# Two-branch attention kernel: when single score tiles may run, when unit queries are loaded, when GpSimd's branch A work pauses

## The chip, the cores and the metric

The kernel runs on one core of one Trainium2 chip. The metric is device time in microseconds of one execution. TensorE multiplies matrices, VectorE (DVE) reduces and combines, ScalarE (ACT) evaluates exponents and copies, GpSimd (POOL) does elementwise work in SBUF, and SyncE (SP) issues most DMAs. Each engine works through its own instructions in the order in which the program lists them.

## What is computed

The reference mixes two attention branches over the same input x (2048 positions, width 512, 32 heads of 16) with a gate per position:

```python
x = A_x
g = _sigmoid((x * gate_w).sum(-1, keepdims=True))
a = _A_ref(x, A_wqkv, A_wo)   # 8 keys per position, at distances 0, 2, ..., 14
b = _B_ref(x, B_wq, B_wk, B_wv, B_wo)
return g * a + (1 - g) * b

# in _B_ref: 32 query heads share one key head and one value head
scores = jnp.einsum("bhqd,bkd->bhqk", q, k) * (Dh ** -0.5)
p = _softmax(scores, axis=-1)
o = jnp.einsum("bhqk,bkd->bhqd", p, v)
```

Branch B is full softmax attention, 32 heads of 2048 x 2048 scores; branch A looks at 8 earlier positions and is done mostly on GpSimd.

## The kernel before

**Units.** Branch B's queries are cut into 32 units, each of 512 queries and 4 heads. A unit is worked off in 16 steps, one for each tile of 128 keys, so that the second phase has 512 steps, `s` from 0 to 511, with `u, kt = divmod(s, 16)`. In a step, `exp_pair` (L568, L570) makes the scores of two heads in each of two PSUM banks `pe` and ScalarE exponentiates them into `pexp`; `weighted(s - 1)` (L578) multiplies the exponents of the step before with the values into the bank `po`.

**Fills.** The exponent is taken of a score less the maximum of its row, and the maxima are needed before the unit's first step. They come from a second pass of score matmuls, which run as fills between the other work. Each unit has 64 of them (2048 in all), each a matmul of 512 columns of keys with half of the array's rows, and a maximum by VectorE; one of these 64 is called a score below. They come in three forms:

- a **pair** (`fill_pair`, L384 and L413): two matmuls on the two halves of the array's rows, into the two-bank tile `pm` (`m2`), reduced in one VectorE instruction;
- a **single** (`fill_one`, L384 and L424): one of two scores of a slot, into the one-bank tile `ps` (`m1`); the other one stands in `half` until the next single. A single can also go through `pm`;
- in the first phase and in the row blocks below, **half forms** (L480, L506, L523), one matmul beside one of the projections.

`slots` lists what is left in order of units, `to_go()` counts it. When a unit's maxima are complete, `maxima_turn`, `shift_a`, `shift_c` and `shift_d` bring them, by way of VectorE and GpSimd (L530 to L541) and eight small DMAs (L556), into rows of the unit's queries.

**Loads of units.** `stack(u)` issues four DMAs on SP (L353, L354) that put a unit's queries from DRAM scratch into a buffer `qst`. There are eight buffers, later six; `home(v)` gives a unit's buffer and the unit whose steps must be over before. `stacked` holds for each unit loaded so far when the planner takes it to have landed (issue plus 5 us); `fillable()` asks that.

**Order.** All of it is one program that is written out in Python with a rough clock for each engine (`clk`, `pool`): the order of instructions on each engine is set by that planner, not by the chip. In each step of the second phase the loop issues: a load, if `s` is past the bound; the first exponent pair; a pair if `m2` is free (`fill_ready("m2", ...)`); a single if `singles(s)` allows it, except in the first step of most units; the second exponent pair; the weighted sum of the step before; then tasks that are due and GpSimd's work. `singles(s)` asks whether pairs in the remaining steps, and PER_ROW scores for each output row still to come, would be too few for what is left.

**Row blocks.** Output rows are made in blocks (`out_phase`, L862): eight rows at step 273, four at step 401 in this kernel. A block starts at the first step of a unit, when the queries' outputs are there and the `lead`, the units' worth of fills done less the units stepped through, is under LEAD = 3.0. The last four rows are spread over the last steps (L933).

**First phase.** `stream` runs the query projections and then branch A's projections: three column groups `gg` of 16 lumps `j`, each lump 12 products `i` on either half of the array's rows (L1185). The weights of the next group are split into two parts (`split_wa`: ScalarE writes `wah`, L111, GpSimd writes `wal`, L112). Two of the four splits are made in the last lump of a group, after its products 4 and 7. `done_mm` calls `run_pool()` after every third product; that issues GpSimd's branch A work (L642 to L702) until its clock is 2.5 us ahead, and with it the exponents and reductions of branch A on ScalarE and VectorE. GpSimd also adds up the projections' stages (L311).

Of the kernel before, what the change touches and what calls it, by code (L numbers as in the profile page):

```python
# [18 lines left out]
NJ = S // P  # L19
# [5 lines left out]
NU = NQB * NHG  # L25
# [8 lines left out]
GG = 3  # L34
GN = NAG * AN // GG
NB = 8
# [2 lines left out]
FMAX = 3.4028234e38  # L39
NH = NJ // 2  # L40
TO_END = 10
LEAD, M2S, M1S, E1S, PER_ROW = 3.0, 0.5, 0.3, 0.2, 20
M2H = 0.15
WB = 6

# [32 lines left out]
def gated_mix_kernel(ctx, tc, xt, wa, wk, wq, wo_a, wo_b, out):  # L78
# [21 lines left out]
    def home(v):  # L100

        return (v % NB, v - NB) if v < 2 * NB - 2 else ((v - NB) % (NB - 2), v - NB + 2)
# [11 lines left out]
    clk = {"pe": 0.0, "act": 0.0, "dve": 0.0}  # L114
# [229 lines left out]
    stacked, asked = [], set()  # L344
# [14 lines left out]
    slots = [(v, pr, t, kc) for kc in range(2) for v in range(2) for pr in range(2) for t in range(4)]  # L359
    slots += [(v, pr, t, kc) for v in range(2) for pr in range(2) for t in range(4) for kc in range(2, 4)]  # L360
    slots += [(v, pr, t, kc) for v in range(2, NU) for pr in range(2) for t in range(4) for kc in range(4)]
    half = []
# [4 lines left out]
    def fillable():  # L367
        return bool(half) or bool(slots) and slots[0][0] < len(stacked) and stacked[slots[0][0]] <= clk["pe"]
# [17 lines left out]
    def to_go():  # L386
        return 2 * len(slots) + len(half)
# [29 lines left out]
    def fill_one(dst=m1, key="m1"):  # L417
        if not half:
            v, pr, t, kc = slots.pop(0)
            half.extend([(v, pr, t, kc, 0), (v, pr, t, kc, 1)])  # L420
        v, pr, t, kc, odd = half.pop(0)
        m = unit_tile(v)
        max_mm(dst, v, pr, t, kc, odd)
        nc.vector.tensor_reduce(m[:, odd, pr, t, kc:kc + 1], dst, AX.X, ALU.max)  # L424
        free[key] = after("dve", after("pe", 0, T_R) + T_LAT, T_RED1) + 0.08
        filled(v, 1)
# [43 lines left out]
    def half_back():  # L470

        nc.sync.dma_start(q67.rearrange("p g x n -> p (g x n)").bitcast(F32), kd.rearrange("p g x n -> p (g x n)"))
        kcd[0] = q67
# [87 lines left out]
    pe, pexp, exped = [], {}, {}  # L561
# [63 lines left out]
    oa, p2, woh, wol = [], [], [], []  # L625
# [345 lines left out]

    def singles(s):

        return 2 * max(0, 16 * (NU - 1) - 16 - s) + PER_ROW * max(0, NJ - 4 - outs) < to_go()

    def fill_ready(key, slack):
        if fillable() and free[key] <= clk["pe"] + slack:
            clk["pe"] = max(clk["pe"], free[key])
            if key == "m1":
                fill_one()  # L980
            elif half and (not slots or half[0][0] < slots[0][0] or slots[0][0] >= len(stacked)):
                fill_one(m2[:, 0, :], "m2")
            elif slots:
                fill_pair(m2, "m2")
# [41 lines left out]
    def run_tasks():  # L1026
        for task in [t for t in tasks if t[0] <= clk["pe"]]:
            tasks.remove(task)
            task[1](*task[2])
# [158 lines left out]
    def done_mm(at):  # L1188
        nonlocal pool
        x, i = at  # L1190
        lump = lumps[x]
        if i % 3 == 2:
            run_tasks()
            if p2:
                run_pool()
        if x == last - 1 and i == 3 * C - 6:
            ended.add(1)
        if lump[0] == "a" and lump[2] == NJ - 1 and lump[1] + 1 < GG and i in (4, 7) and WB - C < 4:
            c = WB - C + (i == 7)
            if c < C:  # L1200
                split_wa(lump[1] + 1, c)
        if x == last and i in (2, 7):
            exp_pair(0, int(i == 7))
        if i < 3 * C - 1:
            return
        if lump[0] == "q":
            m = lump[1]
            if m == 12:
                gates()
            queries_post(m, eb[1 - x % 2])  # L1210
            free[f"e{1 - x % 2}"] = clk["act"]
            ahead_wa(0, m - 4)
        else:
            gg, j = lump[1:]
            a_post(gg, j, 2 if x == last else x % 2)
            if gg + 1 < GG:
                ahead_wa(gg + 1, j - 2)
# [20 lines left out]
    for s in range(NS + 1):  # L1238
        u, kt = divmod(s, NJ)
        if s == 16 * NB + 4:  # L1240
            half_back()
        if len(stacked) < NU and s > 16 * (home(len(stacked))[1] + 1):
            stack(len(stacked))
        if s < NS and kt == 0 and u not in shifted:
            while u not in shifted:
                clk["pe"] += 0.5
                run_tasks()
                if u not in shifted and left.get(u, 1):
                    assert pause(4)
        v = min(x[0][0] for x in (half, slots, [(NU,)]) if x)  # L1250
        need = left.get(v, NF // NU)
        steps = 16 * v - 6 - s
        short = need - 2.8 * max(0, steps) if v < NU else 0
        lead = (NF - to_go()) / 64 - s / 16
        order = (0, "m2", "later") if s else ()
        rows = 4 if outs else 8
        k, n = (outs + rows) // 4 - 1, C - (outs >= NJ - 4)
        if outs == NJ - 4:
            if s in (16 * NU - 40, 16 * NU - 32):
                blocks_out(outs + (s - 16 * NU + 40) // 8)  # L1260
            if to_go() <= 9 and not later_rows and "last" not in done:
                later_rows.append(spread(list(range(outs, NJ)), n))
            if short > 0 and steps < 2:
                pause(short)
        elif due or outs < NJ and s and kt == 0 and outs // NH in done and NHG * (k + 1) - 1 in shaped and (lead < LEAD or s >= 16 * (NHG * (k + 2) + 1)):
            if not due:
                prepare(outs, n)
                due.append(n)
            else:
                out_phase(list(range(outs, outs + rows)), due.pop(), kt == 1)  # L1270
                outs += rows
                order = (0, "m1", 2)
        elif short > 0 and steps < 2:
            pause(short)

        first = 0
        some = min(4, -(-(row_prods[0] - TO_END) // (NS + 1 - s)))
        order = list(order)
        while order:
            which = order.pop(0)  # L1280
            if which == "later":
                order = ["m1", 1] if free["e1"] > clk["pe"] - E1S else [1, "m1"]
                first = 0
            elif which == "m2":
                fill_ready("m2", M2S)
            elif which == "m1":
                if not later_rows and (kt or not s or u >= NU - 8) and singles(s):
                    first = half[0][4] if half else 0
                    fill_ready("m1", M1S)
            elif s < NS:  # L1290
                if which == 1:
                    spread_some(some)
                exp_pair(s, which % 2 or which // 2, which == 2, first)
        if s == NS:
            spread_some(some)
        if s:
            weighted(s - 1)
            if kt == 0 and s < NS:
                finish_a(u - 1, nc.gpsimd)
        run_tasks()  # L1300
        run_pool()
# [65 lines left out]
```

## Time and profile before

| | |
|---|---|
| median of 3 runs | 1475.75 us (1475.53 to 1475.97) |
| the profiled execution, own time | 1475.89 us |
| its span, first to last instruction | 1474.1 us |
| first phase, to the end of the first weighted sum | 273.5 us |
| busy VectorE, ScalarE, GpSimd | 81%, 87%, 68% |

A row of a group names line, engine, operation, what is written and read, shapes and count, then busy time and mean length, then the engine's idle time before it with what ended it. A row of a stretch has its ends, its length, the busy time and count of instructions of each engine (TensorE, its weight loads, and then those of the other engines that take part), the granted TensorE clock as a share of full speed, the share of the DMA engines that is busy, and GB/s. A row of the timeline has start, length, engine, line and operation. `SPq` and the like are an engine's queue, which waits or issues.

### The profile page before, as it was taken

What the parts mean: (1) busy time and instruction counts of PE and PEld (TensorE: products, weight loads), DVE (VectorE), ACT (ScalarE), POOL (GpSimd) and SP (SyncE); (2) the same over time, 40 slices, a digit from 0 to 9 for tenths busy, and PEclk for the clock granted to TensorE, in tenths of its full rate; (3) what the DMA queues carried; (4) which work ended last, traced back from release to release, by engine and by line L of the source; (5) the groups of instructions that cost most, each with busy time, mean ns of one, the idle gap of its engine ahead of it and who ended that gap; (6) DMA issues with size and microseconds to landing.
All of it is one profiled execution on the core that took longest, in us unless ns stands there. A gap on an engine that the chain in (4) does not pass through costs nothing.

```text
span 1474.1 us, 29007 instructions
## 1 busy us (share of the span) xinstructions
PE 1461.2 (99%) x10612; PEld 670.5 (45%) x10612; DVE 1191.0 (81%) x1880; ACT 1289.0 (87%) x1629; POOL 1001.4 (68%) x1753
## 2 busy tenths in 40 slices
PE   9999999999999999999999999999999999999998
PEld 5877777533333333333333377333333354333343
DVE  6978889858888888889898888888888888866612
ACT  5658888999999999999999988999999988999986
POOL 7853888778898988988878898788888231101121
PEclk9999999999999999999999999999999999999999
DMA  6752433211121111211211202021120000000110
GB/s 224 211 161 75 145 100 91 74 56 54 43 96 41 46 58 43 71 42 42 71 42 42 77 28 83 26 71 42 42 71 12 12 19 23 12 1 2 28 32 29
DMA packets 75263, 89.80 MB, mean 61 GB/s; under 512 B 56368, under 2 KB 56416, under 8 KB 70896
## 3 DMA queue, kind: packets, MB, share of 16 engines
q1 hardware_dynamic: 68176, 49.00, 11.7%
q0 software_dynamic: 6368, 37.90, 7.7%
q8 instruction: 83, 1.36, 0.4%
q10 hardware_dynamic: 576, 1.05, 0.2%
q14 instruction: 60, 0.49, 0.1%
HBM read 60.03 MB, written 27.35 MB: 59 GB/s over the span
## 4 chain that ended last, share of the span: by engine, by line
PE 97%; DVE 1%; ACT 1%; issue 1%; POOL 0%; DMA 0%; DVEq 0%; SPq 0%; ACTq 0%; POOLq 0%
PE po L578 34%; PE pe L568 23%; PE pe L1185 11%; PE pm L384 8%; PE ps L384 7%; PE pe L862 5%; PE pm L480 3%; PE po L480 2%; PE ps L480 2%; PE pm L933 1%; PE pe L208 1%; ACT pexp L570 1%; DVE qst L186 0%; POOL wal L112 0%; PE pe L753 0%
## 5 line engine op out<-in xcount | busy, mean ns | idle before, releaser
L570 ACT ACTIVATE pexp<-pe 128x1024 f32<-128x1024 f32 x1022 | 989.4, 1022 | 87.5 <-PE pe L568 84.3
L413 DVE TENSOR_REDUCE mx<-pm 128x2 f32<-128x1024 f32 x491 | 600.9, 1224 | 147.2 <-PE pm L384 136.4
L578 PE MATMUL po<-pexp,vst 128*32 128x512 f32 x4096 | 545.5, 605 | 0.0
L568 PE MATMUL pe<-qst,kst 64*128 64x512 f32 x1916 | 438.7, 451 | 0.8 <-ACT pexp L570 0.7
L568 PEld LDWEIGHTS pe<-qst,kst 64*128 64x128 f32 x1916 | 179.8, 183 | 480.4 <-ACT pexp L570 474.2
L424 DVE TENSOR_REDUCE mx<-ps 128x1 f32<-128x512 f32 x420 | 285.7, 680 | 0.0
L384 PE MATMUL pm<-kst,qst 62*128 62x512 f32 x967 | 196.7, 395 | 1.5 <-DMA qst<-qd 0.8
L642 POOL TENSOR_TENSOR pr<-aext 128x256 f32<-128x256 f32 x256 | 182.2, 739 | 4.5 <-DMA aext<-ad 4.2
L702 POOL TENSOR_TENSOR oa<-oa,av 128x256 f32<-128x256 f32 x224 | 164.0, 732 | 15.2
L384 PE MATMUL ps<-kst,qst 62*128 62x512 f32 x408 | 161.4, 396 | 0.3 <-DVE mx L424 0.2
L578 PEld LDWEIGHTS po<-pexp,vst 128*32 128x32 f32 x4096 | 80.5, 108 | 171.3 <-issue 162.6
L699 POOL TENSOR_TENSOR av<-aext,lg 128x256 f32<-128x256 f32 x224 | 139.3, 622 | 12.6
L506 ACT ACTIVATE dd<-pm 128x512 f32<-128x512 f32 x186 | 104.9, 604 | 23.4 <-PE pm L480 13.1
L1185 PE MATMUL pe<-wal,xh 64*128 64x512 f32 x376 | 118.8, 395 | 1.9 <-POOL wal L112 1.9
L1185 PE MATMUL pe<-wah,xh 64*128 64x512 f32 x376 | 119.8, 397 | 0.0
L1185 PE MATMUL pe<-wah,xl 64*128 64x512 f32 x376 | 118.9, 395 | 0.0
L605 POOL TENSOR_TENSOR rl<-rl,gate_t 128x16 f32<-128x16 f32 x31 | 6.9, 222 | 152.4 <-DVE rl L599 147.6
L384 PEld LDWEIGHTS pm<-kst,qst 62*128 62x128 f32 x967 | 94.0, 187 | 4.4 <-DMA qst<-qd 1.1
L648 POOL TENSOR_TENSOR tr<-pr 128x512 f32<-128x512 f32 x64 | 81.8, 1278 | 4.3
L506 ACT ACTIVATE pexp<-pm 128x512 f32<-128x512 f32 x120 | 68.2, 603 | 13.7 <-PE pm L480 9.5
L384 PEld LDWEIGHTS ps<-kst,qst 62*128 62x128 f32 x408 | 76.1, 187 | 6.4 <-DVE mx L424 3.4
L648 POOL TENSOR_TENSOR tr<-tr 128x256 f32<-128x256 f32 (+1 forms) x128 | 72.4, 565 | 8.8
(215 smaller groups left out, 1975.5 us busy)
## 6 DMA issues: line engine op xcount, KB each, us to landing
aext<-ad POOLq DMA_DIRECT2D x32, 1056.0 KB, 5.5
qst<-qd SPq DMA_DIRECT2D x60, 128.0 KB
ad<-stage SPq DMA_DIRECT2D x32, 240.0 KB
xraw<-xt SPq DMA_DIRECT2D x16, 256.0 KB
qd<-qhi SPq DMA_DIRECT2D x16, 256.0 KB
qd<-qlo SPq DMA_DIRECT2D x16, 256.0 KB
qst<-qd SPq DMA_DIRECT2D x60, 64.0 KB
qst<-ml SPq DMA_DIRECT2D x216, 2.0 KB
```

Of the source, the lines that this page charges most:

```text
L384: nc.tensor.matmul(dst, qst[home(v)[0]][b:b + 62, pr, t * P:(t + 1) * P], kst[b:b + 62, kc * 512:(kc + 1) * 512], start=True, stop=True)
L413: nc.vector.tensor_reduce(m[:, :, pr, t, kc], dst, AX.X, ALU.max)
L424: nc.vector.tensor_reduce(m[:, odd, pr, t, kc:kc + 1], dst, AX.X, ALU.max)
L506: nc.scalar.activation(d[:, odd], m2[:, odd, :], AF.Abs)
L568: nc.tensor.matmul(bank[:, odd, :], kst[b:b + 64, kt * P:(kt + 1) * P], qst[home(u)[0]][b:b + 64, pr, :], start=True, stop=True)
L570: nc.scalar.activation(e, bank, AF.Exp, scale=SCALE)
L578: nc.tensor.matmul(po[32 * i:32 * i + 32, :], vst[:, kt, :], pexp[s, i // 2][:, i % 2, :], start=(kt == 0), stop=(kt == NJ - 1))
L642: nc.gpsimd.tensor_mul(pr[:, k], q, e[:, o:o + NH, AC:2 * AC])
L648: nc.gpsimd.tensor_add(nx, cur[:, :, 0:n], cur[:, :, n:2 * n])
L699: nc.gpsimd.tensor_mul(av, e[:, o:o + NH, 2 * AC:].rearrange("p j (h d) -> p j h d", d=DH), lg[:, w].unsqueeze(3).to_broadcast([P, NH, AG, ...
L702: nc.gpsimd.tensor_add(ao, ao, av)
L1185: nc.tensor.matmul(front[2 if x == last else x % 2][0][:, b, :], l[h], r[h], start=(i == 0), stop=(i == 3 * C - 1))
```

## The change

Four edits, all in the planner:

- `singles(s)` says no while not all units are loaded and the scores ready for fills (of loaded units) are fewer than two for each step until the next unit's load is due and three steps more (`LAND`).
- In `fill_ready`, an odd score in `half` goes through `m2` by itself only if there is nothing left in `slots`, or the next slot's unit isn't loaded or hasn't landed by the planner's clock. Before, it also went so whenever it was of an older unit than the next slot.
- `done_mm` leaves `run_pool()` out from product 8 of lump 14 to product 8 of lump 15, in the first two of the three column groups.
- The loop issues a unit's load from `s >= 16 * (...)` on rather than `s > 16 * (...)`. PER_ROW goes from 20 to 21.

```diff
-LEAD, M2S, M1S, E1S, PER_ROW = 3.0, 0.5, 0.3, 0.2, 20
+LAND = 3
+LEAD, M2S, M1S, E1S, PER_ROW = 3.0, 0.5, 0.3, 0.2, 21
...
     def singles(s):
 
+        if len(stacked) < NU:
+            ready = len(half) + 2 * sum(x[0] < len(stacked) for x in slots[:16 * NB])
+            if ready < 2 * (16 * (home(len(stacked))[1] + 1) + LAND - s) + 1:
+                return False
         return 2 * max(0, 16 * (NU - 1) - 16 - s) + PER_ROW * max(0, NJ - 4 - outs) < to_go()
...
-            elif half and (not slots or half[0][0] < slots[0][0] or slots[0][0] >= len(stacked)):
+            elif half and (not slots or slots[0][0] >= len(stacked) or stacked[slots[0][0]] > clk["pe"]):
                 fill_one(m2[:, 0, :], "m2")
             elif slots:
                 fill_pair(m2, "m2")
...
         if i % 3 == 2:
             run_tasks()
-            if p2:
+            if p2 and not (lump[0] == "a" and lump[1] + 1 < GG and (lump[2] == NJ - 2 and i > 6 or lump[2] == NJ - 1 and i < 9)):
                 run_pool()
...
-        if len(stacked) < NU and s > 16 * (home(len(stacked))[1] + 1):
+        if len(stacked) < NU and s >= 16 * (home(len(stacked))[1] + 1):
             stack(len(stacked))
```

The matmuls, reductions and exponents themselves stay the same; which of them share a slot, and their order, changes.

## The prediction

> **What bounds the kernel now.** I read the page first (busy times, chain of waits), then a timeline of two ordinary steps of the second phase, then stretches of steps, then the few real stalls of TensorE.
>
> ```profile
> span 1474.1 us, 29007 instructions
> PE 1461.2 (99%) x10612; PEld 670.5 (45%) x10612; DVE 1191.0 (81%) x1880; ACT 1289.0 (87%) x1629; POOL 1001.4 (68%) x1753
> PE 97%; DVE 1%; ACT 1%; issue 1%; POOL 0%; DMA 0%; DVEq 0%; SPq 0%; ACTq 0%; POOLq 0%
> ```
>
> TensorE is busy for 99% and carries 97% of the chain. So a change must take matmuls' time, or TensorE's stalls, away. Next, one step of the second phase (start, length, instruction), and ScalarE in a later stretch:
>
> ```profile
> 420.13 0.50 PE L568 MATMUL pe<-qst,kst 64*128 64x512 f32 x2
> 420.47 0.40 PE L384 MATMUL pm<-kst,qst 62*128 62x512 f32 x2
> 420.70 0.41 PE L568 MATMUL pe<-qst,kst 64*128 64x512 f32 x2
> 420.95 0.39 PE L384 MATMUL ps<-kst,qst 62*128 62x512 f32 x1
> 421.27 1.06 PE L578 MATMUL po<-pexp,vst 128*32 128x512 f32 x8
> 422.27 0.50 PE L568 MATMUL pe<-qst,kst 64*128 64x512 f32 x2
> ...
> 1299.83 10.20 ACT L570 ACTIVATE pexp<-pe 128x1024 f32<-128x1024 f32 x10
> ```
>
> A step is two exponent pairs (pe), one fill pair (pm: two matmuls side by side in the array), one single (ps, alone), and the weighted sums (po). It took 2.14 us (420.13 to 422.27). The single occupies TensorE by itself for about a quarter of a microsecond, where a pair takes two scores in the same slot. In steps without a single ScalarE runs without a gap, ten exponents in 10.20 us. Stretches (length, TensorE, weight loads, VectorE, ScalarE, GpSimd, granted clock, DMA):
>
> ```profile
> 273.60:297.20 23.60, 23.60 (x167) 8.52 (x169) 20.34 (x25) 21.84 (x24) 17.78 (x30) 1.00 0.22 70
> 297.20:299.10 1.90, 1.90 (x16) 0.64 (x16) 1.56 (x3) 1.72 (x3) 1.66 (x4) 1.00 0.00 0
> 299.10:311.10 12.00, 11.43 (x74) 3.11 (x74) 1.46 (x4) 11.50 (x13) 9.04 (x16) 1.00 0.39 121
> 311.10:314.30 3.20, 2.40 (x17) 0.84 (x17) 1.24 (x2) 2.50 (x3) 3.12 (x7) 1.00 0.60 188
> 314.30:337.80 23.50, 23.50 (x167) 8.49 (x169) 20.76 (x25) 21.34 (x24) 17.03 (x43) 1.00 0.00 1
> 1276.40:1393.10 116.70, 116.60 (x814) 38.11 (x814) 76.20 (x74) 111.58 (x117) 7.65 (x17) 1.00 0.03 8
> ```
>
> The same stretches for the weighted sums alone (eight records a step) and for the fills alone:
>
> ```profile
> 273.60:297.20 23.60, 11.72 (x88) 1.73 (x88) 1.00 0.22 70
> 299.10:311.10 12.00, 6.39 (x48) 0.94 (x48) 1.00 0.39 121
> 1276.40:1393.10 116.70, 61.79 (x464) 9.12 (x464) 1.00 0.03 8
> ...
> 273.60:297.20 23.60, 8.38 (x33) 4.14 (x35) 1.00 0.22 70
> 299.10:311.10 12.00, 0.00 (x0) 0.00 (x0) 1.00 0.39 121
> 1276.40:1393.10 116.70, 23.13 (x116) 10.95 (x116) 1.00 0.03 8
> ```
>
> Numbered by the loop (the fills of step s run beside the weighted sum of s-1), 273.60 begins step 2. So 11 steps with pair and single, 2 to 12, take 23.60 (2.145 each; the 11 from 314.30 take 2.136); step 13, with a pair alone, takes 1.90; then **six steps, 14 to 19, have no fill at all** and still take 2.00 each, ScalarE's pace; and 58 steps in a row with a pair alone take 116.70/58 = 2.01. A pair is free in a run of such steps; a single costs 2.136 - 2.01 = 0.124 us there, 0.236 beside a lone 1.90. At 299.10 the eight loaded units were used up, since singles ran through steps 1 to 12; step 20, at 311.10, is the first with unit 8.
>
> **Part 1: held singles, the sooner load, and the half that waits.** Fills of the second phase:
>
> ```profile
> L413 DVE TENSOR_REDUCE mx<-pm 128x2 f32<-128x1024 f32 x464 | 568.1, 1224 | 142.4 <-PE pm L384 131.9 <-PE ps L384 6.8
> L424 DVE TENSOR_REDUCE mx<-ps 128x1 f32<-128x512 f32 x395 | 268.8, 680 | 0.0
> ...
> L424 DVE TENSOR_REDUCE mx<-pm x9: 691/692/693, 404.1 to 1149.5; 128x1 f32<-128x512 f32 x9
> ```
>
> From step 2 to step 480 there are 479 places for a pair. 464 are taken; 6 were empty, and 9 held a single only (pm, 128x1: an odd half of an old unit went first, which the edit of the fill rule stops). 464 + 6 + 9 = 479.
>
> At step 1 eight units are loaded and, counting back from 299.10, where they are used up (two scores in step 13, 33 in steps 2 to 12, three in step 1), 38 scores are ready. The new test asks at step s whether ready is under 2*(16+3-s)+1 = 39-2s; after the pair of step s there are 38-2s. It holds by one, at every step to 16: singles stop, pairs last. At step 16 unit 8's load is issued, 8 are left before the step's pair, and singles return at 17. No step is then without a pair: all 479 are used, 15 more. Of the scores that they take, 30, nine are the odd halves; two fewer come to the row blocks (an odd half stood ahead of each); so **19 singles go**. Later the test binds once more, for three steps ahead of step 288.
>
> The stretch 273.60 to 314.30 (steps 2 to 20, 40.70 us): after the change 15 steps with a pair alone at 2.01 = 30.2, and four with both at 2.136 = 8.5; 38.7, so 2.0 less, and 0.1 for step 1's single, that lies before it: **2.1**. That includes the stall at its end:
>
> ```profile
> 274.73 33.13 SPq L556 DMA_DIRECT2D q<-ml  x13
> 307.96 0.62 SPq L353 DMA_DIRECT2D qst<-qd  x1
> ...
> 312.56 0.47 PE L384 MATMUL pm<-kst,qst 62*128 62x512 f32 x1 [0.80 <-DMA qst<-qd]
> ```
>
> Unit 8's four loads stood on SP behind the shift copies (L556) of unit 7, and TensorE waited 0.80 us for them, until 312.56. Now unit 7 ends only at step 18, so its copies come behind the loads. From first issue to use the loads took 312.56 - 307.96 = 4.6 us. They can go once step 15's exponents have read the buffer (about 1.1 us, the weighted sum, before step 16), and are first needed in step 19: 1.1 + 2.0 + 2.1 + 2.1 + 0.5 = 7.8 us. Margin 3.2, no stall.
>
> The other units: moved are four issues of some 0.6 each, past the shift copies and output-weight loads of the same step, which then wait for four issues, 2.4 us; no engine waits for a unit's copies so closely, since fills run two units ahead of the steps. SP stands at the loads' wait beforehand in most cases, so their issue time stays and only the planner's landing time moves.
>
> Nine of the 19 singles lie in that stretch and step 1 (12 before, 3 after). The other **10 at 0.124 are 1.2 us**, in the held steps before 288 and where the singles end, which now is some steps sooner. The nine pairs for singles cost VectorE 1.224 - 0.692 each; it is at 20.34 of 23.60 in a full stretch, so that is hidden (uncovered: 4.8 in all). PER_ROW 21 raises the stop by four scores while four rows are left: that moves singles, and removes none; 0.
>
> Bounds: a step with a pair alone costs between 1.90 and 2.136. At 1.90 the stretch is 37.0 and the ten singles are 2.4: 6.2 together with step 1. At 2.136 it is 40.6 and they are nothing: 0.1. I take 2.01, since the 58-step run is the like case.
>
> **Part 2: the row block may move.** The second block (four output rows, step 401) needs a lead under 3 units. My count at step 400 is
>
> ```profile
> 1191.40:1474.10 282.70, 41.78 (x186) 19.76 (x186) 1.00 0.07 19
> ...
> 1191.40:1474.10 282.70, 24.70 (x76) 13.04 (x76) 1.00 0.07 19
> ```
>
> 186 + 76 = 262 scores to go before (fills, then the block's own fills), a lead of (2048-262)/64 - 25 = 2.91. After: 9 + 3 more done, less 3 held and 1 of the first block, 254: lead 3.03, so the block goes to step 417. Its work is the same and all units are loaded; 0. With three scores more to go it would stay at 401, which is as likely as not, and by the same token costs nothing.
>
> **Part 3: GpSimd pauses.** Stalls of TensorE at the ends of groups 0 and 1:
>
> ```profile
> 138.65 1.30 POOL L112 TENSOR_TENSOR wal<-waraw,wah 128x512 fp32r<-128x512 f32 x1 [4.76 <-ACT wah L111]
> 142.50 0.49 PE L1185 MATMUL pe<-wal,xh 64*128 64x512 f32 x1 [0.39 <-POOL wal L112]
> ...
> 203.90 1.17 ACT L111 ACTIVATE wah<-waraw 128x512 fp32r<-128x512 f32 x2
> 205.06 0.74 POOL L702 TENSOR_TENSOR oa<-oa,av 128x256 f32<-128x256 f32 x1
> 205.76 1.29 POOL L112 TENSOR_TENSOR wal<-waraw,wah 128x512 fp32r<-128x512 f32 x1
> 207.00 1.30 POOL L311 TENSOR_TENSOR stage<-stage,two 128x512 f32<-128x512 f32 x1
> 208.25 1.27 POOL L112 TENSOR_TENSOR wal<-waraw,wah 128x512 fp32r<-128x512 f32 x1
> 209.58 0.49 PE L1185 MATMUL pe<-wal,xh 64*128 64x512 f32 x1 [1.50 <-POOL wal L112]
> ```
>
> At group 0's end GpSimd is idle for 4.76 us: the pause finds nothing and the 0.39 stays. At group 1's end the first split waits for branch A's work (L702) to 205.76, though ScalarE's half is done by some 204.6 (half of 1.17 after 203.90). With the pause it starts 1.1 sooner, the stage sum (L311) still stands between, and the stall falls from 1.50 to 0.4, as at group 0: **1.1 us**. Bounds: 0, if other branch A work is still queued, to 1.9, if both stalls go; -0.5 if the work held (a few operations of 0.7) comes in the way later. It is otherwise covered: GpSimd is busy 68%.
>
> **Sum:** 2.1 + 1.2 + 1.1 = 4.4. The profiled execution took 1475.89 (span 1474.1 and 1.8 around it), 0.14 above the median 1475.75. 1475.9 - 4.4 = **1471.5**.
>
> **Rivals.**
> *The singles were free.* If the held steps run at 2.136, as ScalarE also has branch A's exponents there, part 1 gives 0.1 and the time is 1475.9 - 1.2 = 1474.7. For it: ScalarE busy 21.84 of 23.60. Against: the six steps without fills ran at 2.00 in that very place.
> *TensorE's pace.* 6.2 + 1.9 = 8.1: 1467.8. Against: ScalarE's 10 exponents in 10.20.
> *The sooner load meets branch A's.* Its 1 MB window is issued at 301.1:
>
> ```profile
> aext<-ad POOLq DMA_DIRECT2D x32, 1056.0 KB, 5.5
> ```
>
> 5.5 us to landing. Were unit 8's load put off by all of that, it would take 10.1 where 7.8 are to be had: a stall of 2.3, 1473.8. For it: the load moves from 307.96 to about 302. Against: it is a third of the bytes. The Trainium skill ("DMA: Bandwidth & Descriptors", "Issuing engines are not separate DMA queues") says that transfers from all issuers end on the same 16 DMA engines and interleave; by that rule the load is late by a part of the 5.5, by two own queues by none.
> *Slower: a load stuck on SP.* By the same count 6 scores are left after step 288, in which the next unit's load is issued, so it too has a margin near 3.2. Should a shift copy stand ahead of it whose maxima GpSimd has not yet turned, it waits as these do:
>
> ```profile
> SPq L556 <- POOL ml L541: 213.3, 14, 60.0
> ```
>
> 15.2 on average. Stall 15.2 - 3.2 = 12.0, time 1483.5; it makes the kernel slower once the lateness passes 3.2 + 4.4. For it: unit 8's case before. Against: copies follow a unit's last score, and here that falls behind the load.
>
> **How the numbers follow.** Forecast 0.60, singles free 0.13, TensorE's pace 0.08, load meets branch A 0.09, stuck load 0.10. About 0.2% (2.95 us) is what a measurement of this kernel tells from no change. The forecast's own range is 1470.0 to 1473.0, nearly all faster, and with TensorE's pace this gives 0.68; singles free and the met load lie within 0.2%, with a remainder of the forecast, 0.22; the stuck load 0.10. The range takes the forecast, the two middle rivals and most of the way to the fast bound: 1468.3 to 1476.0.
>
> **What would show it.** Steps 14 to 19 with pairs; 479 pairs after step 1 and no 128x1 reduce from pm; ps reduces down from 395 to about 376; no wait for qst<-qd near 312; the wait for wal at 209 down to about 0.4; the second block 16 steps later. Wrong: steps 2 to 16 at 2.13, a new wait of fills for loads, or empty steps elsewhere.

## The result and the profile after

The changed kernel takes 1473.68 us (median), the kernel before 1475.75: ratio 0.9985, 95% interval 0.9978 to 0.9992. That is 2.07 us faster where 4.25 was forecast. Two of the changed kernel's 20 executions took 1940 us at a granted clock of 0.65 and 0.75 and are left out of the ratio. The profiled execution has a span of 1471.6 (before 1474.1). Its page, busy times and chain of waits:

```profile
span 1471.6 us, 28990 instructions
PE 1461.3 (99%) x10612; PEld 669.0 (45%) x10612; DVE 1189.9 (81%) x1865; ACT 1288.7 (88%) x1629; POOL 1003.5 (68%) x1753
PE 95%; DVE 2%; POOL 1%; issue 1%; ACT 1%; DVEq 0%; POOLq 0%; ACTq 0%
```

TensorE is busy as long as before (1461.3 and 1461.2 us), in a shorter span. The stretches below show that this is a balance: busy time and stalls fell at the start and in the later steps, and the second block is busier. The fills of the second phase, by line:

```profile
L414 DVE TENSOR_REDUCE mx<-pm 128x2 f32<-128x1024 f32 x479 | 586.2, 1224 | 147.3 <-PE pm L385 142.7
L425 DVE TENSOR_REDUCE mx<-ps 128x1 f32<-128x512 f32 x374 | 254.6, 681 | 0.6 <-PE ps L385 0.6
```

All 479 places hold a pair, no odd score runs through `pm` by itself any more, and 21 singles are gone. The time by stretch shows where this paid. Rows are as in the prediction (length, then TensorE, weight loads, VectorE, ScalarE, GpSimd; clock; DMA): steps 2 to 20, the steps up to the first row block, that block and the step behind it, the steps between, the second block and the step behind it, the rest up to step 480. Before:

```profile
273.51:314.30 40.79, 39.42 (x269) 13.21 (x268) 24.68 (x32) 37.65 (x40) 31.60 (x54) 1.00 0.29 90
314.30:848.12 533.82, 533.82 (x3760) 192.38 (x3760) 474.85 (x593) 490.93 (x524) 459.27 (x876) 1.00 0.17 53
848.12:926.07 77.95, 77.43 (x645) 53.40 (x645) 65.94 (x190) 65.54 (x120) 69.96 (x113) 1.00 0.17 58
926.07:1193.45 267.38, 267.38 (x1883) 96.33 (x1883) 237.52 (x295) 245.29 (x261) 193.04 (x355) 1.00 0.12 38
1193.45:1233.71 40.26, 39.47 (x333) 27.12 (x333) 33.55 (x92) 32.45 (x58) 16.03 (x26) 1.00 0.08 28
1233.71:1393.02 159.31, 159.21 (x1115) 53.63 (x1114) 114.20 (x119) 149.99 (x156) 11.57 (x27) 1.00 0.03 8
```

After:

```profile
272.61:311.60 38.99, 38.84 (x273) 13.23 (x272) 26.91 (x29) 37.20 (x40) 28.12 (x47) 1.00 0.33 94
311.60:845.24 533.64, 533.63 (x3764) 192.34 (x3763) 475.98 (x591) 491.10 (x524) 463.95 (x883) 1.00 0.16 53
845.24:923.84 78.60, 77.33 (x643) 53.09 (x643) 66.55 (x186) 63.05 (x116) 69.83 (x113) 1.00 0.17 57
923.84:1224.28 300.44, 300.44 (x2119) 107.92 (x2118) 264.74 (x323) 276.16 (x294) 197.53 (x365) 1.00 0.11 35
1224.28:1265.95 41.67, 41.45 (x338) 28.05 (x338) 34.41 (x99) 34.75 (x62) 14.59 (x23) 1.00 0.09 29
1265.95:1390.48 124.53, 124.53 (x871) 39.98 (x870) 81.32 (x78) 119.91 (x125) 9.45 (x21) 1.00 0.03 7
```

Forecast and measured, in us of the span:

| term | forecast | measured | from |
|---|---|---|---|
| first phase, up to the first weighted sum | -1.1 | -0.90 | 272.61 - 273.51 |
| steps 2 to 20, with step 1's single | -2.1 | -1.80 | 38.99 - 40.79 |
| ten later singles | -1.2 | -1.90 | 533.64 - 533.82, and 300.44 + 124.53 - 267.38 - 159.31 |
| first row block and the step behind it | 0 | +0.65 | 78.60 - 77.95 |
| second row block and the step behind it | 0 | +1.41 | 41.67 - 40.26 |
| tail | 0 | -0.01 | |
| sum | -4.4 | -2.55 | |

The start and the singles did what was forecast. **Two terms that the forecast put at nothing, the row blocks, took back 2.06 us.** Each stretch is from one profiled execution, so the spread between executions of equal plans matters. The first block with its step took 78.60, 78.57, 78.49 and 78.19 in four executions with the changed kernel's plan for it, and 77.95, 77.92 and 77.77 in three with the plan before. The second took 41.67, 41.60 and 41.59 in three with the plan of the changed kernel. So both terms are more than spread. The experiments ask why, and what the pause, the hold and the sooner load are worth by themselves. Each was timed beside the kernel before on its own chip (1475.88 to 1476.02 us there).

### The profile page after: what moved, and what is told of

It is laid out like the page before. It is cut to its first block, busy times and chain, and to the rows that moved or that the text cites. A ratio compares the mean times of both kernels' runs of the same rounds, so it can differ in the third digit from the quotient of the medians.

```text
span 1471.6 us, 28990 instructions
## 1 busy us (share of the span) xinstructions
PE 1461.3 (99%) x10612; PEld 669.0 (45%) x10612; DVE 1189.9 (81%) x1865; ACT 1288.7 (88%) x1629; POOL 1003.5 (68%) x1753
## 4 chain that ended last, share of the span: by engine, by line
PE 95%; DVE 2%; POOL 1%; issue 1%; ACT 1%; DVEq 0%; POOLq 0%; ACTq 0%
PE po L579 35%; PE pe L569 24%; PE pe L1190 10%; PE pm L385 8%; PE ps L385 6%; PE pe L863 4%; PE pm L481 2%; PE ps L481 2%; PE po L481 2%; PE pm L934 1%; PE pe L209 1%; DVE qst L187 0%; POOL wal L113 0%; DVE pexp L524 0%; POOL qlo L255 0%
## 5 line engine op out<-in xcount | busy, mean ns | idle before, releaser
L414 DVE TENSOR_REDUCE mx<-pm 128x2 f32<-128x1024 f32 x506 | 619.1, 1223 | 152.1 <-PE pm L385 147.4
L569 PE MATMUL pe<-qst,kst 64*128 64x512 f32 x1916 | 440.4, 453 | 0.2
L569 PEld LDWEIGHTS pe<-qst,kst 64*128 64x128 f32 x1916 | 179.7, 183 | 482.2 <-ACT pexp L571 477.1
L425 DVE TENSOR_REDUCE mx<-ps 128x1 f32<-128x512 f32 x399 | 271.5, 680 | 0.6 <-PE ps L385 0.6
L385 PE MATMUL ps<-kst,qst 62*128 62x512 f32 x397 | 157.2, 396 | 0.2 <-DVE mx L425 0.2
L524 DVE CUSTOM_DVE_ANT_0 dd<-ps,dd 128x512 f32<-128x512 f32 x93 | 64.2, 690 | 15.8 <-PE ps L481 8.7
```

The lines of the kernel that those rows point to most:

```text
L385: nc.tensor.matmul(dst, qst[home(v)[0]][b:b + 62, pr, t * P:(t + 1) * P], kst[b:b + 62, kc * 512:(kc + 1) * 512], start=True, stop=True)
L414: nc.vector.tensor_reduce(m[:, :, pr, t, kc], dst, AX.X, ALU.max)
L569: nc.tensor.matmul(bank[:, odd, :], kst[b:b + 64, kt * P:(kt + 1) * P], qst[home(u)[0]][b:b + 64, pr, :], start=True, stop=True)
```

## Experiments on the second block: its place or its size

**The block back at step 401.** The edit to the changed kernel:

```diff
-LEAD, M2S, M1S, E1S, PER_ROW = 3.0, 0.5, 0.3, 0.2, 21
+LEAD, M2S, M1S, E1S, PER_ROW = 3.1, 0.5, 0.3, 0.2, 21
```

> The changed kernel with LEAD 3.1 for 3.0, so that the second row block starts at step 401 again, as in the kernel before, now on a slot boundary and with 88 scores in it (79 before, 84 in the changed kernel). The block and the step after it took 40.26 us before and 41.67 in the changed kernel. Theory P, the later place costs: back to 40.3 us, time 1473.7 - 1.4 = 1472.3. Rival S, a block costs more the more scores it takes in, (41.67 - 40.26)/5 = 0.28 us each: 40.26 + 9 x 0.28 = 42.8 us, against which four fewer singles after it save 0.5; time 1474.3.

Measured: 1475.22 us, ratio 0.9994 (0.9985 to 1.0004). Most of the gain is gone. Its second block and next step:

```profile
1191.33:1234.80 43.47, 41.53 (x342) 27.70 (x341) 34.47 (x99) 35.72 (x64) 15.88 (x25) 1.00 0.08 27
```

The one long wait in it, in the timeline of TensorE and of GpSimd:

```profile
1199.96 0.49 PE L863 MATMUL pe<-woh,turned 64*128 64x512 f32 x1 [0.99 <-POOL turned L768]
...
1196.35 2.26 POOL L557 DMA_DIRECT2D qst<-ml  x4 [0.34 <-POOL ml L542]
1198.63 1.28 POOL L768 TENSOR_TENSOR turned<-raw,turned 128x512 fp32r<-128x512 f32 x1
```

The block grew at its old place too, with 88 scores by 3.21 us against before's 79 (43.47 - 40.26). A later place (theory P) is not the cost. Size (S) has the right sign and too small a figure: it gave 42.8. Part of the growth is an accident of order: a unit's maxima came just then, its four copies took GpSimd 2.26 us, and the operand of the second output row (`turned`, L768), queued behind them, kept TensorE waiting 0.99 us. With nine scores at the 0.13 to 0.17 us found below, and this wait, 0.7 to 1.0 of the 3.21 stays open.

**The kernel before with its block moved to 417** (LEAD 2.9 in the kernel before, nothing else).

> The kernel before with LEAD 2.9 alone: the second row block goes to step 417 and takes in 83 scores for 79. Theory P (later place): block and next step 41.7 us for 40.26, time 1475.75 + 1.4 = 1477.1. Rival S (0.28 us a score): 40.26 + 4 x 0.28 = 41.4 us, less four singles of 0.124 after it; time 1476.4. If neither: 40.3 us and 1475.7.

Measured: 1476.09, ratio 1.0001 (0.9991 to 1.001). Block and next step:

```profile
1228.05:1268.97 40.92, 40.52 (x337) 27.35 (x337) 35.40 (x98) 33.81 (x60) 14.32 (x23) 1.00 0.08 28
```

The block is at 40.92 where P gave 41.7 and S 41.4. Four scores more (83) cost 0.66 at the new place, 0.165 each; four singles fewer gave 0.4 back (426.31 against 426.69 for the steps outside the blocks). So a score moved from a step into a block saves nothing. The changed kernel's 84 cost 41.67, 0.75 above this for one score more: size alone isn't all.

**One more single before the first block.** By the planner's count, which the fills in the trace bear out, the changed kernel came to the first block with 793 scores left, one of a slot's two done and the next slot off a boundary of key blocks, and half forms, which go by key blocks in twos, began 6.8 us into the block (2.7 before). This run lets one single more through at step 272:

```diff
-                if not later_rows and (kt or not s or u >= NU - 8) and singles(s):
+                if not later_rows and (kt or not s or u >= NU - 8 or s == 272) and singles(s):
```

> The changed kernel with one more single at step 272, so that the first row block starts with nothing in half and an even key quarter: its half forms can begin at once. The block took 75.51 us before (164 half-form matmuls, TensorE idle 0.74) and 76.33 in the changed kernel (156, idle 1.54). Theory A, a start off the boundary costs the block time (pairs in slots of their own, then waits): 75.5 us or less, at most 76.0, time 1473.0 with the single's 0.24 paid. Rival S, what counts is the number of scores taken in (172 for 165 now): over 77 us, time 1474 or more.

Measured: 1473.04, ratio 0.998 (0.9971 to 0.9989). First block with its next step:

```profile
845.43:924.00 78.57, 77.24 (x650) 54.53 (x650) 66.68 (x196) 66.65 (x124) 69.43 (x113) 1.00 0.16 57
```

The first block takes as long (78.57, 78.60) but does 172 scores instead of 165; the later steps need 8 singles fewer, and the span falls by 0.60 to 1471.0. The time is theory A's, but its block is not: by itself it took 76.34 us, over A's limit of 76.0. The block does more in the same time instead of ending sooner. Before's block did 167 scores in 77.95; five more at 0.13 to 0.17 make 78.6 to 78.8, what is measured here. So the starting state of the first block cost about 0.6 us at the end of the span, the size of the first block's +0.65.

## Experiments on how a block ends

At the end of the changed kernel's second block (TensorE's timeline):

```profile
1260.09 0.63 PE L863 MATMUL pe<-woh,turned 64*128 64x512 f32 x4
1260.55 0.40 PE L481 MATMUL ps<-q,qst 62*128 62x512 f32 x1
1261.15 0.50 PE L481 MATMUL po<-q,qst 62*128 62x512 f32 x1 [0.20 <-DVE mx L524]
1261.15 0.74 PE L569 MATMUL pe<-qst,kst 64*128 64x512 f32 x2
```

The row products (L863) end, a half form (L481) is left over, the last one waits for VectorE, and only with it come the exponents' scores (L569). This is called the drain below. In the kernel before, the first of the exponents' scores ran beside the last row product:

```profile
1228.78 0.39 PE L568 MATMUL pe<-qst,kst 64*128 64x512 f32 x1
1228.78 0.39 PE L862 MATMUL pe<-woh,turned 64*128 64x512 f32 x1
```

**Half forms ended sooner, second block alone** (in the changed kernel; the last row then begins no group once nine products are left):

```diff
-            if x == len(js) - 1 and i == m - 5:
+            if x == len(js) - 1 and i == m - (5 if len(js) > 4 else 9):
```

> The changed kernel, but in the second row block no new half-form group begins once the last row has only nine (instead of five) products left: 80 scores in the block instead of 84, still at step 417, the first block unchanged. Theory D (part of the block's extra time is its end: the last half forms are drained alone after the last row product, so the next step's exponents start 0.8 us late): half forms end with or before the last row product, block and next step go from 41.67 to about 40.4 us (0.7 for the drain, 4 scores at 0.13 for their slots), 4 scores more in the later steps cost 0.5 to 0.65; median 1473.0 to 1473.3. Rival Q (a block costs its scores and nothing else, half a 0.255 us slot each): block and next step about 41.15, later steps +0.5 to +0.65, median 1473.6 to 1473.9.

Measured: 1472.97, ratio 0.9981 (0.9972 to 0.999). Its end:

```profile
1260.65 0.62 PE L863 MATMUL pe<-woh,turned 64*128 64x512 f32 x3
1261.11 0.41 PE L569 MATMUL pe<-qst,kst 64*128 64x512 f32 x2
...
1263.85 0.50 PE L385 MATMUL pm<-kst,qst 62*128 62x512 f32 x2 [0.42 <-ACT pexp L571]
```

The block with its next step:

```profile
1225.04:1265.82 40.78, 40.27 (x335) 27.45 (x334) 32.79 (x93) 33.45 (x60) 13.34 (x19) 1.00 0.09 31
```

The drain is gone: the exponents start 36.07 us into the block instead of 36.87. But 0.42 of that returns one step later as a wait for ScalarE. Block and step fall by 0.89, between the two theories' figures. Four scores fewer are 0.52 at 0.13 us (an estimate: half of the quarter of a microsecond that a pair takes) and 0.66 at the 0.165 measured above, so the drain is worth 0.2 to 0.4 net. The later steps pay 0.59 for the four singles (300.52 + 125.04 against 300.44 + 124.53).

This run's span isn't below the changed kernel's (1471.9 and 1471.6), although its median is. The cause is its start, which is planned alike: TensorE waited for unit 8's queries, which it hadn't in the changed kernel:

```profile
308.35 0.47 PE L385 MATMUL pm<-kst,qst 62*128 62x512 f32 x1 [0.27 <-DMA qst<-qd]
```

**Both blocks, with the single at step 272** (the changed kernel with that edit and `i == m - 9` for all blocks).

> The changed kernel with one more single at step 272 (so that the first block starts on a boundary of key blocks) and with half-form groups ended nine products before the end in both row blocks. Theory D: each block and its next step lose the drain, 0.5 to 0.7 us net of the scores that move out, so 0.8 to 1.3 us under the 1473.04 of the run with the one single: 1471.8 to 1472.3. Rival Q: 1472.9 to 1473.2.

Measured: **1470.48, ratio 0.9966 (0.9953 to 0.9978)**, the fastest of all and under the range of theory D. First and second block with next step:

```profile
846.07:922.03 75.96, 75.00 (x643) 54.06 (x642) 64.22 (x188) 64.41 (x120) 67.07 (x108) 1.00 0.16 55
...
1222.88:1263.30 40.42, 39.98 (x334) 27.25 (x334) 32.88 (x93) 33.46 (x60) 13.35 (x19) 1.00 0.09 31
```

The first block and its step lose 2.61 us for eight half forms fewer (1.0 to 1.3 of it); the rest, 1.3 to 1.6, is more than theory D had put on the drain. The later steps pay 1.38 for twelve more singles (300.85 + 125.06 against 300.01 + 124.52). The five executions lie between 1470.32 and 1471.34, and the profiled one (1471.22) is among the slow ones, so its stretches show the gain rather too small.

**The same end in the kernel before** (`i == m - 9`, nothing else).

> The kernel before with one edit that the change does not have: no new half-form group begins in the last row of a block once nine (instead of five) products are left. Theory D (a block that ends with half forms alone pays for it, whichever kernel): before's first block ends with two half forms after its last row product, its second with none. So the first block and its next step shorten by 1.3 to 2.7 us, the second by under 0.4, the scores moved out cost 0.5 to 1.0 in the later steps; median 1474.0 to 1474.9. Rival N (the end costs only what the change itself brought): first block within 0.5 us of 77.95 less the slots of the scores that leave it, median 1475.5 to 1476.0.

Measured: 1475.57, ratio 0.9996 (0.9987 to 1.0005). The time says rival N, the first block says D (first row; then the stretch behind the second block):

```profile
848.22:924.16 75.94, 75.21 (x639) 52.55 (x638) 63.34 (x184) 63.60 (x118) 68.11 (x110) 1.00 0.17 59
...
1232.20:1392.68 160.48, 160.47 (x1122) 54.25 (x1122) 119.21 (x128) 150.57 (x156) 11.59 (x27) 1.00 0.03 8
```

First block and step fall by 2.01 (77.95 before), but the eight scores that leave the blocks come back as singles and cost 1.17 in the last stretch (160.48 against 159.31) and 0.3 in the one between. Before's second block had no drain to lose: it took 40.34 with its step, against 40.26, though four scores left it, so the price of a score in a block isn't one figure. The drain is no fault of the change, then; what the change brought is a second block that ends in one.

**Both ends, and singles held until unit 8's queries are in** (changed kernel, `i == m - 9`, and):

```diff
     def singles(s):
 
+        if len(stacked) == 9 and stacked[8] > clk["pe"]:
+            return False
```

> The changed kernel with half-form groups ended nine products before the end of each block, and with no singles while unit 8's queries are under way (in two runs TensorE waited 0.15 to 0.27 us at 308 us for them). By that the first block starts on a boundary of key blocks with 792 scores left, the second comes at step 401 on a boundary with 256 left. Theory D with size: first block about 73 us, second and its next step about 39.9 to 40.5, no wait for the queries at 308 to 312 us; median 1469.8 to 1470.8. Rival (step 401 is a worse place than 417 for the same 80 scores): second block and next step over 41.5, median over 1471.5.

Measured: 1471.85, ratio 0.9971 (0.996 to 0.9982), one above the range of theory D and above the rival's bound, but the stretches are D's:

```profile
845.50:921.28 75.78, 75.20 (x638) 54.23 (x638) 62.80 (x184) 63.87 (x118) 68.49 (x110) 1.00 0.17 59
...
1189.41:1228.89 39.48, 39.02 (x331) 26.66 (x331) 31.92 (x92) 32.71 (x60) 16.01 (x26) 1.00 0.09 30
```

No wait for queries, and 80 scores at step 401 in 39.48 us: the place is not worse than 417 (40.42 for 80), and what makes it 0.94 better is open. A later place as the cost falls for good; state at the start and drain at the end stand.

## Experiments on the start

**The hold alone** (in the kernel before; fetch still at `s >`, no pause):

```diff
+        if len(stacked) < NU:
+            ready = len(half) + 2 * sum(x[0] < len(stacked) for x in slots[:16 * NB])
+            if ready < 2 * (16 * (home(len(stacked))[1] + 1) + LAND - s) + 1:
+                return False
```

> The kernel before with the holding back of singles alone: unit queries still fetched at step 18 of their turn, no pause of GpSimd, the same 36 ready scores. Both row blocks then meet the list of score blocks in the same state as in the kernel before (799 scores left at the first, 259 at the second, at step 401). Theory T (start and row blocks are separate terms): steps 2 to 20 shorten by 1.6 to 1.9 us (40.78 before, 38.99 after), both row blocks stay within 0.15 us of before (75.51 + 2.44 and 37.22 + 3.04), so all the gain of the start reaches the end: span 1472.2 to 1472.5, median 1473.8 to 1474.1. Rival L (the stall at the start ends only when the queries also come a step sooner): steps 2 to 20 shorten by under 0.6 us, median 1475.2 to 1475.8.

Measured: 1474.23, ratio 0.9989 (0.998 to 0.9998). SyncE's fetch in the timeline:

```profile
300.31 0.61 SPq L354 DMA_DIRECT2D qst<-qd  x1
```

Steps 2 to 20, and the second block with its next step:

```profile
272.95:311.71 38.76, 38.60 (x270) 12.98 (x269) 25.20 (x27) 37.05 (x40) 27.85 (x46) 1.00 0.31 95
...
1191.50:1232.05 40.55, 39.47 (x333) 27.05 (x333) 33.46 (x92) 32.56 (x58) 16.08 (x26) 1.00 0.08 28
```

Theory T is right in the main: the hold by itself brings 2.03 us at the start (40.79 to 38.76), and rival L falls. The median is 0.13 above T's range, and the second block moved by 0.29, where T allowed 0.15. The fetch leaves at 300.31, not 307.96 as before, though its step is unchanged: unit 7's copies, which stood ahead of it on SyncE, now come later (at 312.60). With block states as before, the blocks cost about what they cost before (77.77 and 40.55 against 77.95 and 40.26). The steps up to the first block took 0.6 longer (534.42), for which nothing in their plan accounts. The first phase is 0.56 shorter, which the hold can't have done (last section). Of the 0.56 and the start's 2.03 together 1.63 reached the end of the span.

**The sooner fetch alone** (kernel before, `s >=` for `s >`).

> The kernel before with the unit queries fetched one step sooner and nothing else: singles are not held, no pause. The fetch of unit 8's queries then stands ahead of unit 7's copies in SyncE's queue instead of behind them. Theory P (the queue place sets when the fetch goes out; in the run with the hold alone the fetch left at 300.3 us without being a step sooner): the fetch leaves at 299.9 to 300.6 us instead of 307.96, the stall of 0.80 us at 311.8 is gone, steps 2 to 20 shorten by 0.7 to 1.2 us (less than with the hold, since the singles of steps 2 to 12 stay). But the second block then moves to step 417 and takes 88 scores: by the size theory it and its next step take 42.3 to 43.5 us instead of 40.26, for nine scores that saved about 1.3 us as singles, so the end gains little: median 1475.2 to 1476.4. Rival H (only the hold ends the stall): steps 2 to 20 within 0.3 us of 40.78.

Measured: **1489.61, ratio 1.009 (1.0074 to 1.0105)**. Both theories are wrong. The timeline of SyncE, then of TensorE:

```profile
303.04 5.20 SPq L556 DMA_DIRECT2D q<-ml  x8
308.35 0.62 SPq L353 DMA_DIRECT2D qst<-qd  x1
...
311.53 0.49 PE L384 MATMUL pm<-kst,qst 62*128 62x512 f32 x1 [1.56 <-DMA qst<-qd]
313.25 0.76 PE L384 MATMUL pm<-kst,qst 62*128 62x512 f32 x1 [1.22 <-DMA qst<-qd]
```

Steps 2 to 20:

```profile
273.88:318.48 44.60, 41.23 (x272) 13.76 (x271) 26.71 (x34) 37.40 (x40) 35.19 (x66) 0.96 0.25 83
```

The fetch still stands behind unit 7's copies, since unit 7 ends as soon as before. The planner takes it to have landed a step sooner, so fills come sooner, and TensorE waits 2.8 us for them; steps 2 to 20 take 3.8 more. The wait isn't all: from about its end on the granted clock is at half for 3.4 us, and eight weighted-sum products that take 1.06 us elsewhere took 1.93 (at 314.40). The same comes once more behind step 480, where TensorE waits for the operand of an output row, which had waited for a DMA:

```profile
312.80:316.30 3.50, 3.05 (x14) 0.77 (x14) 1.82 (x2) 1.02 (x1) 3.34 (x5) 0.51 0.29 111
...
1422.69 0.79 PE L933 MATMUL pm<-woh,turned 64*128 64x512 f32 x2 [2.79 <-POOL turned L910]
...
1422.20:1429.00 6.80, 6.31 (x28) 2.38 (x30) 0.00 (x0) 2.80 (x3) 3.28 (x5) 0.50 0.20 40
```

TensorE was busy for 3.05 + 6.31 us at half the clock, so by an estimate some 4.7 us of the loss are the clock's. In the other profiled executions the clock is full until the last matmuls, also after a single wait of 1.50 us (in the run without the pause, below). Of the span's 15.2 us, 4.4 lie in the first block with its step (176 half forms, 82.37 us, TensorE idle for 2.2 of them, 0.5 before), 1.5 in the second and 4.8 behind step 480; why the first block took so long was not followed up. The sooner fetch does no such harm in the change, where the hold makes unit 7 end late.

## Experiments on the pause

**The pause alone**, in the kernel before:

```diff
-            if p2:
+            if p2 and not (lump[0] == "a" and lump[1] + 1 < GG and (lump[2] == NJ - 2 and i > 6 or lump[2] == NJ - 1 and i < 9)):
                 run_pool()
```

> The kernel before with GpSimd's pause alone. If its share is what the traces show, the first phase ends 0.9 us sooner (the wait for wal near 209 falls from 1.50 to 0.4 us, and 0.4 of another gap near 162 goes) and everything after it runs as before: 1474.85 us. Rival: the pause's gain is given back in branch A's later work: 1475.5 or more.

Measured: 1475.63, ratio 0.9998 (0.9988 to 1.0007): the rival's figure, not the 1474.85 expected. **Without the pause**, the changed kernel and the fastest version (both ends, single at step 272):

> The changed kernel without GpSimd's pause at column-group ends; steps and row blocks are planned exactly as in the changed kernel. Theory G (most of the stall that the pause removes at 207 us is given back at 223 to 231 us, where VectorE sums half forms back to back): the wait at 207.7 is 1.4 to 1.6 us again, first weighted sum ends 0.3 to 0.5 us later than in the changed kernel (272.61), median 1473.95 to 1474.2. Rival F (the forecast: the removed stall counts in full): first weighted sum 1.0 to 1.2 us later, median 1474.7 to 1474.9. The wait of 0.4 to 0.5 us for ScalarE's copy at 160.8 us, which the kernel before has and the changed one has not: if it returns, the pause removed it; if not, the run's layout did.

> The best version so far (the changed kernel, one more single at step 272, half-form groups ended nine products before the end of each block; 1470.48 us) without GpSimd's pause. Two pairs so far disagree on the pause: the first weighted sum came 0.30 and 0.48 us sooner with it, but the whole kernel was 0.30 us faster with it in one pair and 0.58 us slower in the other, where the first row block was 0.42 us shorter without it. Theory G (the pause is worth its net 0.3 to 0.5 us of the first phase, the rest is the spread between runs): first weighted sum at 272.95 to 273.2 instead of 272.62, first block within 0.15 us of 73.10, span 1469.7 to 1470.0, median 1470.7 to 1471.1. Rival B (the pause hands GpSimd's work on to the first row block and loses there what it gained): first block 72.6 to 72.8, span within 0.15 us of 1469.43, median 1470.0 to 1470.5.

Measured: 1473.10, ratio 0.9982 (0.9973 to 0.9991), and 1471.85, ratio 0.9972 (0.996 to 0.9983). TensorE's wait for the weight split, in the timeline of the run with the pause alone:

```profile
208.38 0.49 PE L1185 MATMUL pe<-wal,xh 64*128 64x512 f32 x1 [0.42 <-POOL wal L112]
```

In the changed kernel:

```profile
208.07 0.49 PE L1190 MATMUL pe<-wal,xh 64*128 64x512 f32 x1 [0.40 <-POOL wal L113]
```

In the changed kernel without it:

```profile
209.14 0.50 PE L1190 MATMUL pe<-wal,xh 64*128 64x512 f32 x1 [1.50 <-POOL wal L113]
```

The stall falls from 1.50 to 0.40 as forecast, and TensorE resumes 1.07 sooner (208.07 against 209.14). By the first weighted sum 0.48 is left (272.61 and 273.09). In the pair of the fastest version it is 0.28 (272.62 and 272.90), with the pause alone 0.45 (273.06 against 273.51), of which some 0.1 was there before the stall. The expectation put the loss at 223 to 231 us, and that is wrong: it has happened by 214. The same copy of ScalarE in the changed kernel, then without the pause:

```profile
214.44 0.59 ACT L303 ACTIVATE stage<-pe 128x512 f32<-128x512 f32 x1
...
214.88 0.59 ACT L303 ACTIVATE stage<-pe 128x512 f32<-128x512 f32 x1
```

The lead is 0.44 here and stays between 0.42 and 0.49 on ScalarE up to 271 us; in the pair of the fastest version it is 0.31 at this copy, with the pause alone 0.53. In between, ScalarE waits 0.50 and 0.31 us for half forms in the changed kernel, and 0.27 without the pause. What sets the pace there isn't settled. Over the whole kernel the three pairs are 0.30 and 1.37 us faster with the pause and 0.58 slower; the spans 0.08 and 0.42 faster and 0.33 slower. The intervals of the changed kernel's pair overlap, so do those of the fastest version's, and with the pause alone the interval holds 1. The first block, planned alike, ran 0.42 us shorter without the pause in one pair and 0.65 longer in the other, so B falls: nothing is handed on to it. G's worth at the start is borne out, its figures for the whole kernel are not (1473.95 to 1474.2 and 1470.7 to 1471.1). The pause's worth is 0.3 to 0.5 us in its own phase, and no more than the spread between runs at the end.

## Why the prediction was right in direction and too large

The forecast of 1471.5 was 2.2 us too fast.

- **Bound.** Right: TensorE's share and clock are as before, and every gain was a stall or an unshared slot.
- **Held singles.** Right in mechanism and nearly in size: all 479 places filled, steps 14 to 19 with pairs, 21 singles fewer (19 forecast), -1.80 for 2.1. The hold alone makes it. The three held steps forecast ahead of step 288 did not come: outside the block no step from 21 to 287 is without a single, but for the first of each unit, as before.
- **Later singles.** 13 fewer behind step 20 and outside the blocks, not 10, at 1.90/13 = 0.146 each, near the 0.124 of the forecast.
- **The sooner load's margin.** The forecast gave 3.2 us; there was hardly any. The fetch issued at 299.99 was in time at 307.61 in the changed kernel, but in the run with the second block's end alone it was first used at 308.35 after an issue at 300.07, 8.3 us where the kernel before needed 4.6. Issue and first use in the changed kernel:

```profile
299.99 0.62 SPq L354 DMA_DIRECT2D qst<-qd  x1
...
307.61 0.53 PE L385 MATMUL pm<-kst,qst 62*128 62x512 f32 x2
```

That is the rival in which the load meets branch A's window, at a price of 0 to 0.5 instead of 2.3: steps 2 to 20 took 38.99 in the changed kernel, 39.53 and 39.42 in two runs planned alike. The rule that the prediction named from the Trainium skill ("DMA: Bandwidth & Descriptors", "Issuing engines are not separate DMA queues") agrees: the load was late by a part of the window's 5.5 us, 3.0 to 3.7. The DMA engines were 100% busy from 300 to 306 us in the changed kernel, where before's load met them 50% busy (308 to 313). Two loads of output weights, 256 KB each, stand in the same stretch, and no run parts them from the window. That the measured 1473.68 is near this rival's 1473.8 is chance: the changed kernel has no such stall.
- **The stuck load.** It did not come in the change; the fetch alone shows a load stuck behind shift copies one edit away.
- **The pause.** Mis-sized: the stall went as forecast, 1.1, but 0.3 to 0.5 arrived. Some 0.45 of the first phase's -0.90 is from a wait that no edit touches (below).
- **The row block, "Its work is the same and all units are loaded; 0": the step that failed.** The rows of the block are the same, but the block is also where fills run as half forms, and how many it takes, the state in which it starts and how it ends are set by the count of scores left, which the other edits change. Measured +1.41: five more scores at 0.13 to 0.17 (0.65 to 0.85), the drain at 0.2 to 0.4 net, and the rest, some 0.35, open. Nor would staying at step 401 have cost nothing, as the prediction has it: there the block grew by 3.21. The first block wasn't in the sum at all: +0.65, by its start off a boundary.

The gap of the sum is 1.85 us (4.4 - 2.55): the blocks are 2.06 of it, start and first phase 0.5, and the later singles took 0.7 off.

## What to carry to other kernels

Where work is packed by a planner, an edit that moves a few items shifts the state in which every later packed region starts and ends; price those regions by their own rows, as even a block of "the same work" moved by 0.6 to 1.4 us here. Look at the end of a packed region for filler work that runs alone after the main work, and stop feeding it sooner: four products sooner brought 1.5 us of span here on top of a mended start, where the whole change brought 2.5. But count what comes back elsewhere: in the kernel before, the same edit took 2.0 us out of the first block and the time stayed the same (0.9987 to 1.0005). And measure edits alone: one of four that looked harmless costs 13.6 us without its neighbour, in part because TensorE's granted clock fell to half with its waits.

## What was not expected of the hardware

A wait of ScalarE before it copies a projection at 160 us comes and goes. That is ahead of every edit: up to 201 us the engines' instructions are the same, in the same order. The wait is in the profile of the kernel before (0.52 us), of the pause alone (0.40) and of the fetch alone (0.88), each time put down to another engine or line, and in none of the other executions. The timeline of ScalarE in the kernel before:

```profile
160.86 0.60 ACT L302 ACTIVATE stage<-pe 128x512 f32<-128x512 f32 x1 [0.52 <-PE pe L1185]
```

The same copy in the kernel before with sooner ends of its blocks, which is alike up to there:

```profile
160.31 0.59 ACT L302 ACTIVATE stage<-pe 128x512 f32<-128x512 f32 x1
```

The changed kernel's projections are 0.45 us ahead of the kernel before's from there on. That is a fifth of what the whole change gained, and no part of it: from one pair of traces, half a microsecond can't be credited to an edit here.
